# A spectral mixer with a tanh-shrink network: another front for the pipeline, and another way to bound |h|

**Chip, cores, metric.** One core of one Trainium2 chip. The metric is the device time of one execution in microseconds (us), median of several runs. A program on one core has no second die to compare with; all runs told of here were classed as fast.

## The reference

```python
# x: (8, 3008, 256) float32; filt_r, filt_i: (1505, 256) float32
X = np.fft.rfft(x, axis=1)
y = np.fft.irfft(X * (filt_r + 1j * filt_i)[None], n=3008, axis=1).astype(np.float32)
t = y.reshape(24064, 256)
h = t @ w_in                    # w_in: (256, 2048), float64 as it arrives
g = h - np.tanh(h)
out = (g @ w_out).astype(np.float32)   # w_out: (2048, 256), float64
```

## The kernel before

The length 3008 is split as 64 x 47. A batch's transform has a first step (`first`: `x` to `a`, stored to a scratch tensor `ct1`), a middle step (`middle`: `pz`, times the filters into `uv` and `zs`, then `pe`, stored to `ct2`), and a last step (`last`: `pu`, copied into `ut`). The first batch has its own form of these, the **front**. Then the main loop runs 192 units. Each has seven products instead of eight in `up` (h in blocks, by sums of blocks), the shrink function, and seven products in `down`; the sums are made by GpSimd (`combine`). The transforms of later batches are threaded through the loop. TensorE is meant to be busy all the time.

The weights arrive as 64-bit floats, and the kernel rebuilds them from their bits as 32-bit ones, in eight quarters of two jobs each. Five quarters are converted in the front, three in the loop's first units:

```python
def converted(tiles, src, dsts, queue):
    # ... t = raw 64-bit words, loaded on SP
    yield
    V.tensor_scalar(out=it, in0=hi, ...)                 # mantissa bits
    ACT.activation(ft, it, AF.Identity, bias=1.0, scale=2.0 ** -20)
    V.tensor_scalar(out=pt, in0=hi, ...)                 # exponent
    ACT.activation(pt, pt, AF.Relu, bias=exp_b)
    V.tensor_scalar(out=st, in0=hi, ...)                 # sign
    V.scalar_tensor_tensor(out=ft, in0=lo, scalar=2.0 ** -52, in1=ft, ...)
    yield
    V.tensor_scalar_min(pt, pt, 255.0)
    # ... two to four more VectorE operations, into wu or wd

# in the front:
ws = weights(tiles0, range(5), 2)           # advanced by next(ws) in first0 and in each step j
# in the loop:
late, copies = weights(tiles1, range(5, 8), 2), filters_d()
# ...
if k in (0, 2, 4):
    next(late, None)
elif U > 0:
    next(copies, None)                      # 8 x 6 DMAs on SP, filters into a DRAM scratch
```

The shrink uses an approximation that holds for |h| < 0.98. A bound of |h| is computed on the chip, and a general path runs if it fails. The bound is |W|^T max|u|: a reduce after each `last`, and at the end the absolute weights and 64 small matmul passes:

```python
V.tensor_reduce(out=largest[:, :, i:i + 1], in_=ut[:, :, 0:n], axis=X, op=ALU.max,
                apply_absolute_value=True)               # 48 times
# shrink, twice a unit:
ACT.activation(y[k], ht[k], AF.Arctan, scale=S)
ACT.activation(y[k], y[k], AF.Square)
# bounded(), in the last four units and after them:
#   w_abs = |wu[0:2]|, |wu[4] + wu[3]|, |wu[3]|     (ScalarE, VectorE, 8 steps)
#   pb = w_abs^T @ largest ; small = pb < NEAR ; least = min ; count = ones^T @ least
```

`turned`, in the front, prepares the second half of an inverse matrix (`gx`) with two ScalarE operations for each of eight chunks.

Of the kernel before, what the change touches and what calls it, by code (L numbers as in the profile page):

```python
# [41 lines left out]
EARLY = 3  # L42
# [101 lines left out]
def kernel(  # L144
# [32 lines left out]
    largest = cst.tile([128, 2, len(groups)], F32, name="largest")  # L177
# [14 lines left out]
    def converted(tiles, src, dsts, queue):  # L192
# [13 lines left out]
        ACT.activation(ft, it, AF.Identity, bias=1.0, scale=2.0 ** -20)  # L206

        V.tensor_scalar(out=pt, in0=hi, scalar1=20, scalar2=0x7FF,
                        op0=ALU.logical_shift_right, op1=ALU.bitwise_and)
        ACT.activation(pt, pt, AF.Relu, bias=exp_b)  # L210
        V.tensor_scalar(out=st, in0=hi, scalar1=-2 ** 31, scalar2=None, op0=ALU.bitwise_and)
        V.scalar_tensor_tensor(out=ft, in0=lo, scalar=2.0 ** -52, in1=ft,
                               op0=ALU.mult, op1=ALU.add)
        yield
        V.tensor_scalar_min(pt, pt, 255.0)
# [10 lines left out]
    def weights(tiles, quarters, ahead):  # L226

# [21 lines left out]
        def start(k):  # L249
            j = converted(tiles, *jobs[k], nc.sync)  # L250
            next(j)
            return j

        def sums(u):
            w = (wu if u < 4 else wd)[:, :, 256 * (u % 4):256 * (u % 4) + 256]
            G.tensor_sub(w[:, 4], w[:, 6], w[:, 3])
            G.tensor_sub(w[:, 5], w[:, 4], w[:, 0])
            G.tensor_sub(w[:, 2], w[:, 1], w[:, 5])
            G.tensor_sub(w[:, 6], w[:, 0], w[:, 6])

        began = [start(k) for k in range(ahead)]
        yield
        for k in range(len(jobs)):
            next(began[k])
            if k and k % 2 == 0:
                sums(quarters[k // 2 - 1])
            if k + ahead < len(jobs):
                began.append(start(k + ahead))
            yield
            next(began[k])  # L270
            yield
        sums(quarters[-1])
        yield

# [57 lines left out]
    def load_a2(p, j, filters=True):  # L332

        t = tr.tile([RP2, 2 * BD], F32, tag="a2", bufs=2, name="a2")
        row = 32 * len(UNITS[p]) * DM
        nc.sync.dma_start(t, dram(ct1[p], 2 * j * BD, [[row, RP2], [1, 2 * BD]]))
        n = 2 if len(UNITS[p]) == 2 else 4
        if not filters:
            return t
        ft = tr.tile([128, 2, n, DM], F32, tag="ft", bufs=2, name="ft")  # L340
        for p0 in (0, IM):
            nc.sync.dma_start(ft[p0:p0 + IM], dram(filt_d, n * j * DM,
                                                   [[2 * NK * DM, IM], [NK * DM, 2], [1, n * DM]]))
        if n * (j + 1) == NK:
            nc.sync.dma_start(ft[IM:IM + 1, 0, n - 1, :],
                              dram(filt_r.tensor, SEQ // 2 * DM, [[DM, 1], [1, DM]]))
        return t, ft
# [61 lines left out]

    CHUNKS = [chunks_of(bs, CH) for bs in UNITS]  # L410
# [26 lines left out]
    def last(i, z):  # L437
# [7 lines left out]
        for h in range(2):  # L445
# [5 lines left out]
            if h == 0:  # L451
                yield
        V.tensor_reduce(out=largest[:, :, i:i + 1], in_=ut[:, :, 0:n],
                        axis=mybir.AxisListType.X, op=ALU.max, apply_absolute_value=True)
# [73 lines left out]
    def shrink(U):  # L528
# [9 lines left out]
        def start(k):  # L538
            y[k] = tiles("y", 2)
            ACT.activation(y[k], ht[k], AF.Arctan, scale=S)  # L540
            ACT.activation(y[k], y[k], AF.Square)  # L541
# [145 lines left out]
    def bounded(z):  # L687


        ng = len(groups)  # L690
        small = tr.tile([128, 2, NP, ng], F32, tag="a2", bufs=2, name="small")
        ones = cst.tile([128, 1], F32, name="ones")
        G.memset(ones, 1.0)
        w_abs = [tr.tile([128, 2, DFF // 2], F32, tag="ft", bufs=2, name="w_abs")
                 for _ in range(2)]
        for half in range(2):
            for t in range(4):
                cols = slice(t * 256, (t + 1) * 256)
                if half == 0:
                    ACT.activation(w_abs[0][:, :, cols], wu[:, 0:2, cols], AF.Abs)  # L700
                else:
                    V.tensor_add(w_abs[1][:, 0, cols], wu[:, 4, cols], wu[:, 3, cols])
                    ACT.activation(w_abs[1][:, 0, cols], w_abs[1][:, 0, cols], AF.Abs)
                    ACT.activation(w_abs[1][:, 1, cols], wu[:, 3, cols], AF.Abs)
                yield
        for half in range(2):
            pb = z("pb", [128, NP, ng])
            for t in range(NP):
                for h in range(2):
                    nc.tensor.matmul(pb[:, t], w_abs[half][:, h, t * 128:(t + 1) * 128],  # L710
                                     largest[:, h], start=(h == 0), stop=(h == 1),
                                     skip_group_check=True)
                if t == NP // 2 - 1 and half == 0:
                    yield
            V.tensor_single_scalar(out=small[:, half], in_=pb, scalar=NEAR, op=ALU.is_lt)
            if half == 0:
                yield
        least = cst.tile([128, 1], F32, name="least")
        V.tensor_reduce(out=least, in_=small, axis=mybir.AxisListType.XYZ, op=ALU.min)
# [3 lines left out]
        yield  # L723
# [69 lines left out]
    with tc.tile_pool(name="tr", bufs=2) as tr:  # L793
        with tc.tile_pool(name="pro", bufs=1) as pro, \
# [7 lines left out]
            def big(shape, dtype, name):  # L802

                return pro.tile(shape, dtype, tag="big", bufs=4, name=name)
# [35 lines left out]
            def filters_of(c, to=None):  # L840


                n = 4 if c < NK // 4 - 1 else 3

                def put(row, m, v, i, n_s, src, off, dims):
                    if to is None:
                        dst = t[IM * v + row:IM * v + row + m, v, i:i + n_s, :]
                    else:
                        dst = dram(to, ((row * 2 + v) * NK + 4 * c + i) * DM,
                                   [[2 * NK * DM, m], [DM, n_s], [1, DM]])  # L850
                    (G if to is None else nc.sync).dma_start(dst, dram(src.tensor, off, dims))

                if to is None:
                    t = filt[c % 3]


                    if c < 3:
                        for v in range(2):
                            G.memset(t[IM * v + 32:IM * v + 64, v], 0.0)
                    if n == 3:  # L860
                        G.memset(t[IM:IM + 1, 1, 3], 0.0)
                for row, m in ((0, LO), (LO, 16), (LO + 16, HI - 16)):
                    sign = 1 if row < LO else -1
                    r0 = 4 * c + 1 + NQ * row if row < LO else NQ * (row - LO + 1) - 1 - 4 * c
                    for v, src in enumerate((filt_r, filt_i)):
                        put(row, m, v, 0, n, src, r0 * DM, [[NQ * DM, m], [sign * DM, n], [1, DM]])
                if n == 3:
                    for v, src in enumerate((filt_r, filt_i)):
                        put(v, LO - v, v, 3, 1, src, v * NQ * DM,
                            [[NQ * DM, LO - v], [DM, 1], [1, DM]])  # L870
                        put(LO, HI, v, 3, 1, src, NQ // 2 * DM,
                            [[NQ * DM, HI], [DM, 1], [1, DM]])
                return None if to is not None else t
# [8 lines left out]
            def turned(g3, t):  # L882


                ACT.copy(t[0:RP], g3[IM:IM + RP])
                ACT.mul(t[IM:IM + RP], g3[0:RP], -1.0)
# [11 lines left out]
            with tc.manual_schedule():  # L898
                nc.sync.dma_start(wf1, wf1_d)
                V.memset(near_b, B)  # L900
                V.memset(exp_b, -896.0)
                xs = [load_x0(0, (0, 4, 8)), load_x0(1), load_x0(2)]
                ws = weights(tiles0, range(5), 2)

                pad = pro.tile([64, DM], F32, name="pad")
                G.memset(pad, 0.0)
                G.dma_start(dram(ct1[0], NR * 64 * DM, [[DM, 64], [1, DM]]), pad)
                fts = {0: filters_of(0)}
                gx = [pro.tile([IM + RP, 4, RP2], F32, name=f"gx{k}") for k in range(2)]
                for t in gx:  # L910
                    G.memset(t[32:64], 0.0)
                mats = {0: load_slots(0, pro)}
                next(ws)
                for c in range(3):
                    for k, _ in enumerate(first0(xs[c], c)):
                        if k == 3 or k == 1 and c > 0:
                            next(ws)
                G.dma_start(s2, s2_d)
                fts[1] = filters_of(1)
                a2 = {0: load_a2(0, 0, False)}  # L920
                mats[1] = load_slots(1, pro)
                next(ws)
                double_filters(fts[0], 0)
# [216 lines left out]
```

## Time and profile before

| | before |
|---|---|
| median | 2852.3 us |
| TensorE busy | 2744.0 of 2850.8 us (96%) |
| VectorE, ScalarE, GpSimd busy | 70%, 66%, 61% |
| first `pu` matmul (front's end) | 116.3 us |
| unit 0, 8, 188 (the add into `h` from `y`) | 125.3, 262.7, 2775.5 us |

Read the busy rows first, for where TensorE is not full. Then cut the span by stage, and in each stage ask which wait ends last. A unit is marked by its first VectorE add (`h<-y,s`), which occurs once per unit.

### The profile page before, as it was taken

The numbers are of one execution on the slowest core, as the hardware profiler recorded it, in microseconds if no ns is written. First come the engines' busy times: TensorE is split into PE (matmuls) and PEld (weight loads), VectorE is DVE, ScalarE is ACT, GpSimd is POOL, SyncE is SP. The second block draws the span as 40 slices with busy tenths as digits, with TensorE's granted clock in tenths as the row PEclk, the third lists the DMA queues.
The fourth block names the chain that finished last, engine by engine and source line by source line (L and its number), as shares of the span: only waits on it lengthen the run. The fifth ranks groups of instructions, "written<-read, shape, count | busy, mean of one in ns | idle before, by whom it ended". The sixth has DMA issues, their size and how long they took to land.

```text
span 2850.8 us, 36441 instructions
## 1 busy us (share of the span) xinstructions
PE 2744.0 (96%) x12482; PEld 2276.7 (80%) x12482; DVE 1983.7 (70%) x2211; ACT 1871.5 (66%) x2450; POOL 1738.0 (61%) x1381
## 2 busy tenths in 40 slices
PE   5789999999999999999999999999999999999998
PEld 2567777888878887888877788788888888898887
DVE  4675666766766777766776777676687777777876
ACT  3655666666666666666666667666666666666665
POOL 4345777544677767644576776755466666555554
PEclk7989999999999999999999999999999999999999
DMA  9644443232223322132232223212222322111010
GB/s 265 190 152 118 113 113 92 60 93 84 73 67 80 85 73 59 41 98 78 67 99 67 70 71 83 53 39 68 58 65 62 78 55 57 30 19 25 16 22 16
DMA packets 324269, 217.53 MB, mean 76 GB/s; under 512 B 225037, under 2 KB 276485, under 8 KB 323882
## 3 DMA queue, kind: packets, MB, share of 16 engines
q1 hardware_dynamic: 269304, 160.36, 23.1%
q10 hardware_dynamic: 52818, 51.53, 6.0%
q0 software_dynamic: 1952, 3.22, 0.5%
q8 instruction: 100, 1.64, 0.2%
q14 instruction: 95, 0.78, 0.1%
HBM read 138.87 MB, written 79.17 MB: 76 GB/s over the span
## 4 chain that ended last, share of the span: by engine, by line
PE 77%; ACT 8%; DVE 6%; issue 3%; DMA 3%; POOL 1%; SPq 1%; ACTq 1%; DVEq 0%; POOLq 0%
PE o L591 31%; PE x L484 20%; PE z L484 9%; PE y L484 5%; PE pe L365 3%; PE pu L448 3%; PE pz L384 3%; ACT y L540 2%; PE pf L305 2%; DVE h L545 2%; ACT y L541 1%; DVE uv L399 1%; ACT zs L398 1%; ACT u L490 1%; DMA filt<-in_filt_i_dram 1%
## 5 line engine op out<-in xcount | busy, mean ns | idle before, releaser
L591 PE MATMUL o<-t,wd 128*128 128x256 f32 (+2 forms) x3072 | 775.8, 375 | 0.0
L545 DVE TENSOR_TENSOR h<-h,y 128x1024 f32<-128x1024 f32 (+2 forms) x384 | 582.1, 1516 | 258.1 <-ACT y L541 258.1
L591 PEld LDWEIGHTS o<-t,wd 128*128 128x128 f32 x3072 | 580.6, 190 | 71.7
L484 PE MATMUL x<-tu,wu 128*128 128x256 f32 (+2 forms) x2304 | 591.6, 379 | 18.4 <-ACT u L490 16.9
L549 DVE SCALAR_TENSOR_TENSOR h<-sq,h 128x1024 f32<-128x1024 f32 (+2 forms) x384 | 569.9, 1484 | 20.8 <-ACT y L540 0.5
L463 POOL TENSOR_TENSOR t<-h 128x512 f32<-128x512 f32 (+2 forms) x192 | 240.7, 1253 | 558.9 <-DVE h L549 495.9
L591 PE MATMUL o<-h,wd 128*128 128x256 f32 (+2 forms) x2304 | 581.1, 375 | 0.2 <-DVE h L549 0.2
L484 PEld LDWEIGHTS x<-tu,wu 128*128 128x128 f32 x2304 | 429.4, 191 | 161.5 <-issue 73.3
L591 PEld LDWEIGHTS o<-h,wd 128*128 128x128 f32 x2304 | 430.9, 190 | 70.9 <-issue 19.1
L546 ACT ACTIVATE sq<-y,near_b 128x1024 f32<-128x1024 f32 (+2 forms) x384 | 435.4, 1134 | 6.1 <-DVE h L549 1.4
L540 ACT ACTIVATE y<-h 128x1024 f32<-128x1024 f32 (+2 forms) x384 | 400.0, 1042 | 14.8 <-ACT e L368 7.6
L541 ACT ACTIVATE y<-y 128x1024 f32<-128x1024 f32 (+2 forms) x384 | 399.3, 1040 | 12.2
L490 ACT COPY s<-x 128x512 f32<-128x512 f32 (+2 forms) x192 | 110.8, 577 | 439.8 <-PE x L484 431.2
L466 POOL TENSOR_TENSOR t<-t,h 128x512 f32<-128x512 f32 (+2 forms) x192 | 308.8, 1608 | 0.1
L490 ACT COPY u<-x 128x512 f32<-128x512 f32 (+2 forms) x384 | 219.4, 571 | 68.6 <-PE x L484 33.3
L464 POOL TENSOR_TENSOR t<-h,t 128x512 f32<-128x512 f32 (+2 forms) x192 | 241.7, 1259 | 15.1
L465 POOL TENSOR_TENSOR t<-h 128x512 f32<-128x512 f32 (+2 forms) x191 | 250.2, 1310 | 0.0
L400 POOL TENSOR_TENSOR zs<-zs,ft 128x512 f32<-128x512 f32 x112 | 165.9, 1481 | 117.4 <-ACT zs L398 117.3
L401 POOL TENSOR_TENSOR uv<-uv,zs 128x512 f32<-128x512 f32 x112 | 214.9, 1919 | 15.6 <-DVE uv L399 7.2
L484 PE MATMUL x<-ut,wu 128*128 128x256 f32 (+2 forms) x768 | 198.8, 381 | 8.1 <-DVE h L520 6.5
L500 DVE TENSOR_TENSOR h<-y,s 128x512 f32<-128x512 f32 (+2 forms) x192 | 130.2, 678 | 96.2 <-PE y L484 86.0
L484 PE MATMUL z<-tu,wu 128*128 128x256 f32 (+2 forms) x768 | 194.5, 376 | 0.1
(120 smaller groups left out, 3289.1 us busy)
## 6 DMA issues: line engine op xcount, KB each, us to landing
a<-ct SPq DMA_DIRECT2D x64, 384.0 KB
ct<-e ACTq DMA_DIRECT2D x128, 192.0 KB
ft<-filt SPq DMA_DIRECT2D x96, 256.0 KB
out_dram<-ot SPq DMA_DIRECT2D x1392, 16.0 KB
ct<-a ACTq DMA_DIRECT2D x80, 256.0 KB
x_sb<-in_x_dram SPq DMA_DIRECT2D x69, 256.0 KB
e<-ct SPq DMA_DIRECT2D x33, 512.0 KB
fg<-fg SPq DMA_DIRECT2D x40, 392.0 KB
```

Of the source, the lines that this page charges most:

```text
L463: G.tensor_sub(t[0], b[0][1], b[0][0])
L464: G.tensor_sub(t[1], b[1][1], t[0])
L465: (V if shared else G).tensor_sub(t[2], b[1][1], b[0][1])
L466: G.tensor_sub(t[3], t[1], b[1][0])
L484: nc.tensor.matmul(bank[:, k], wu[:, q - 1, (2 * u + k) * 128:(2 * u + k + 1) * 128], rhs[q - 1], start=(first and k == 0), stop=True, ski ...
L490: ACT.copy(t, X)
L540: ACT.activation(y[k], ht[k], AF.Arctan, scale=S)
L541: ACT.activation(y[k], y[k], AF.Square)
L545: V.tensor_mul(ht[k], ht[k], y[k])
L546: ACT.activation(sq[k], y[k], AF.Square, bias=near_b, scale=A)
L549: V.scalar_tensor_tensor(out=ht[k], in0=sq[k], scalar=K, in1=ht[k], op0=ALU.add, op1=ALU.mult)
L591: nc.tensor.matmul(product(q), wd[:, q - 1, (2 * u + k) * 128: (2 * u + k + 1) * 128], rhs[q - 1][:, k], start=(u == 0 and k == 0 and q == ...
```

## The change

Its intent: the front is one that a sibling kernel uses. VectorE converts three quarters alone, before the first batch's middle step; three more follow in the steps; the last two come in the loop in small steps, with ScalarE's part one step behind VectorE's. `turned` moves to GpSimd, the filters' copies to GpSimd in ten DMAs (the largest of 744 rows of 1 KB), `e` gets four buffers, one early `first` step fewer. And |h| is bounded by the sums of y = arctan(S h)^2 that ScalarE's accumulator gives beside the squares: if every sum is under arctan(S 0.98)^2, every |h| is under 0.98. The diff below is cut; it leaves out, among other things, that `a2` is loaded a chunk further ahead and that one hand-written order of instructions now spans the whole program, where the front and the loop had one each.

```diff
-EARLY = 3
+EARLY = 2
@@ converted(..., alone=False)
         V.tensor_scalar(out=it, in0=hi, scalar1=0xFFFFF, ...)
-        ACT.activation(ft, it, AF.Identity, bias=1.0, scale=2.0 ** -20)
         V.tensor_scalar(out=pt, in0=hi, scalar1=20, ...)
-        ACT.activation(pt, pt, AF.Relu, bias=exp_b)
         V.tensor_scalar(out=st, in0=hi, scalar1=-2 ** 31, ...)
+        yield
+        if alone:
+            V.tensor_scalar(out=ft, in0=it, scalar1=2.0 ** -20, scalar2=1.0, ...)
+            V.tensor_scalar(out=pt, in0=pt, scalar1=-896.0, scalar2=0.0, ...)
+        else:
+            ACT.activation(ft, it, AF.Identity, bias=1.0, scale=2.0 ** -20)
+            ACT.activation(pt, pt, AF.Relu, bias=exp_b)
+        yield
# ... (more yields; weights() interleaves two jobs; weights_alone(), weights_slow() are new)
@@ the front
-                ws = weights(tiles0, range(5), 2)
+            ws = weights_alone(tiles0, range(3))
# ...
+            a2[1] = load_a2(0, 1, False, "ft")
             double_filters(fts[0], 0)
+            for _ in ws:
+                pass
+            ws = weights(tiles0, range(3, 6), 2)
@@ turned
-                ACT.copy(t[0:RP], g3[IM:IM + RP])
-                ACT.mul(t[IM:IM + RP], g3[0:RP], -1.0)
+                G.tensor_copy(t[0:RP], g3[IM:IM + RP])
+                G.tensor_scalar_mul(t[IM:IM + RP], g3[0:RP], -1.0)
@@ the loop
-                for c in range(NK // 4):
-                    filters_of(c, filt_d)                # six DMAs each, on SP
+                for v, row, m, i, n, src in filter_rows(0, NK):
+                    G.dma_start(dram(filt_d, ...), src)  # ten DMAs in all
                     yield
-            late, copies = weights(tiles1, range(5, 8), 2), filters_d()
+            late, copies = weights_slow(tiles1, range(6, 8)), filters_d()
@@ the bound
-        V.tensor_reduce(out=largest[:, :, i:i + 1], in_=ut[:, :, 0:n], ...)
-            ACT.activation(y[k], y[k], AF.Square)
+            ACT.activation(y[k], y[k], AF.Square,
+                           accum_out=y_sums[:, 2 * U + k // 2:2 * U + k // 2 + 1])
-        # w_abs, pb: eight steps of ScalarE and VectorE, 32 matmuls
+        V.tensor_single_scalar(out=small, in_=y_sums, scalar=float(np.arctan(S * NEAR) ** 2),
+                               op=ALU.is_lt)
+        V.tensor_reduce(out=least, in_=small, axis=mybir.AxisListType.X, op=ALU.min)
         pc = z("pc", [1, 1])
         nc.tensor.matmul(pc, least, ones, start=True, stop=True)
# called in unit total + 1, k == 0: between the last products
```

## The prediction

> **What bounds the kernel now.** I read the page's busy shares and forty slices first. They show where TensorE is short of its best.
>
> ```profile
> PE 2744.0 (96%) x12482; PEld 2276.7 (80%) x12482; DVE 1983.7 (70%) x2211; ACT 1871.5 (66%) x2450; POOL 1738.0 (61%) x1381
> ...
> PE   5789999999999999999999999999999999999998
> ...
> PEclk7989999999999999999999999999999999999999
> DMA  9644443232223322132232223212222322111010
> ```
>
> TensorE is busy 2744.0 of 2850.8 us, so all its idle time is 106.8 us. It lies in the first slices and the last one (a slice is 71 us). The clock is below full only there too. I then cut the span by stage in the view of windows: the front of batch 0 (0 to 119 us; the first `pu` matmul starts at 119.0), the first units of the main loop, the middle, and the tail.
>
> ```profile
> 0.00:44.00 44.00, 16.82 (x26) 6.00 (x26) 12.05 (x26) 14.59 (x24) 18.19 (x33) 0.82 0.93 271
> 44.00:103.00 59.00, 48.58 (x178) 32.24 (x178) 46.26 (x89) 37.17 (x56) 32.88 (x54) 0.87 0.90 233
> 103.00:119.00 16.00, 9.27 (x29) 5.24 (x29) 1.26 (x3) 4.00 (x7) 1.89 (x3) 0.83 0.58 177
> 119.00:262.00 143.00, 124.84 (x493) 96.48 (x494) 98.64 (x125) 83.22 (x112) 59.36 (x55) 0.91 0.47 143
> 262.00:500.00 238.00, 222.55 (x909) 166.03 (x908) 144.44 (x161) 162.41 (x223) 186.44 (x133) 0.99 0.41 106
> 500.00:2780.00 2280.00, 2263.55 (x10530) 1916.30 (x10529) 1635.49 (x1754) 1534.47 (x1978) 1409.84 (x1083) 1.00 0.25 62
> 2780.00:2850.80 70.80, 58.42 (x324) 54.43 (x322) 45.52 (x57) 35.62 (x54) 29.43 (x25) 0.95 0.08 16
> ```
>
> The columns are the stretch, its length, busy time of PE, PEld, DVE, ACT and POOL, granted clock, DMA share, GB/s. From 500 to 2780 us TensorE idles 16.5 us in 2280. It is the bound there, and nothing that VectorE, ScalarE or GpSimd is spared there can buy more than that. In the first 103 us the sixteen DMA engines are 90 to 93% busy: the front is held by transfers, with waits of ScalarE and VectorE among them. From 119 to 262 us TensorE idles 18.2 us and runs at 0.91 of its clock. That is the softest place.
>
> The waits of the front name the culprits. Columns: who waited, for whom, us in total, times, longest.
>
> ```profile
> DVE conv L205 <- DMA raw<-in_moe_w_in_dram: 21.6, 1, 21.6
> ACT conv L206 <- DVE conv L205: 16.5, 4, 7.9
> PE pf L828 <- ACT a L831: 9.5, 2, 5.8
> PE pz L952 <- DMA a<-ct: 9.3, 1, 9.3
> ACT a L306 <- PE pf L305: 6.8, 2, 6.4
> ```
>
> ScalarE takes its work in order. It stands at the first conversion, which waits for raw weights that land at 22.5 us, and only then copies batch 0's `pf` out of PSUM.
>
> From 105 to 300 us the waits of TensorE and of the SP queue say the same of the late quarters:
>
> ```profile
> PE x L484 <- ACT u L490: 12.5, 5, 3.8
> PE pf L305 <- DMA x_sb<-in_x_dram: 10.9, 4, 5.4
> ...
> SPq L198 <- DVE ft L212: 30.6, 4, 12.4
> SPq L851 <- DMA ct<-a: 24.1, 7, 6.6
> ```
>
> SP stands behind raw loads whose buffer isn't free and behind the filters' copies (L851). The `x` loads queue behind them. ScalarE's `u` copies stand behind conversions.
>
> **What the Trainium skill says.** (1) "TensorE: Matmul & The Clock Gate", Part 1: an idle window drops the array to half clock, and it must be busy some 3.4 us to get it back. The trace agrees: x4 matmul groups of 1.03 us take 2.07 us after the 3.61 us wait at 141 us. The mean clock 0.987 means some 2 x 0.0125 x 2851 = 71 us at half clock, nearly all before 281 us. (2) "DMA: Bandwidth & Descriptors", "Issuing engines are not separate DMA queues": transfers from SP, ScalarE and GpSimd share the same 16 engines, so moving an issue saves only time on the issuing queue. The front's 0.90 to 0.93 fits, so I count nothing for bytes. (3) "ScalarE: Activation LUTs", "What ACT_TABLE_LOAD costs": an ACTIVATE costs 186 ns + 0.833 ns per element, 93 ns more with a pointer bias. For 1024 elements 1039 and 1132 ns; the trace has 1040 (L541) and 1134 (L546). The page says an accumulator output exists, but no price; no row of before shows one. (4) "Perfetto Trace Analysis", "DMA Instruction — SWDGE (GPSIMD)": GpSimd's part of a DMA is writing descriptors. Its filter loads here take 0.56 us each (L851), with 28 to 96 rows of 1 KB alike.
>
> **The change part by part.**
>
> *First stage on VectorE alone.* Six of sixteen half-quarter conversions no longer use ScalarE (two activations, 0.63 + 0.71 us each, out of ten such in the old front). VectorE gets two more simple passes of 0.43 us. One job is then 5 x 0.43 + 2 x 0.69 + 0.76 = 4.3 us of VectorE without a hand-over. ScalarE's `pf` copies no longer wait: of the 9.5 us wait most goes, and `a<-ct` can start some 8 us earlier. But the six jobs take 6 x 4.3 = 26 us of VectorE after the first raw weights land at 22.5, so its first `uv` comes at about 49 to 50 us against 46.2 now. The early start is largely given back there.
>
> *The middle of batch 0.* It holds 6 conversions instead of 7, `turned` leaves ScalarE (8 x 1.03 us) for GpSimd, `e` gets four buffers for two (11.1 us of ScalarE waits for `ct<-e`), and `a2` is loaded a step earlier. Steps now take 59/16 = 3.7 us. When nothing waits they take 3.0 (pz and pe of 84 to 91 us). 16 x 3.1 from 50 us ends at about 100. DMA load rises by one quarter, 1 MB, some 4 us at 250 GB/s. So I count 2 us here, not 8.
>
> *The gap from 103 to 119.* The third early `first` step waits for `x_sb` (5.4 us), then for a buffer of `a1`, and ScalarE stands with it (`ACT ut L450 <- DMA ct<-a` 2.2 us). With EARLY = 2 and the loads begun a step earlier this goes: 7 us. Front together: **9 us** (0 to 15).
>
> *The loop's first units.* Two quarters instead of three come late, in small steps in which ScalarE's part is issued one step after VectorE's. The filters' copies, 48 issues and more on SP, become 10 on GpSimd. What there is to win from 119 to 300 us: idle 24 us, and clock: 34 us at half clock, of which some 28 busy, cost 14. Together 38. GpSimd's ten issues, if 0.6 to 3 us, are 6 to 30 us of an engine busy 59 of 143 us there. I take 40% of 38: **15 us** (5 to 25).
>
> *The bound.* Before: 48 reduces of 1.22 us on VectorE (59 us), 64 matmuls and 8 steps of absolute weights. After: an accumulator read after each of 384 squares. Estimated at 0.1 to 0.25 us each from the fixed part of an activation, that is 40 to 95 us of ScalarE, taking it from 1535/2280 = 67% to some 70%. Both lie beside TensorE. VectorE's release and the lengthened chain `y` to `h` (258 us of waits by VectorE, hidden) about cancel: **0** (-5 to +5).
>
> *The tail.* In the timeline, two batches of 16 `pb` matmuls stand between `o` products, and 32 more stand behind the last transposes:
>
> ```profile
> 2825.15 1.88 PE L710 MATMUL pb<-largest,w_abs 128*128 128x48 f32 x16
> 2828.45 1.88 PE L710 MATMUL pb<-largest,w_abs 128*128 128x48 f32 x16
> 2837.91 3.67 PE L710 MATMUL pb<-largest,w_abs 128*128 128x48 f32 x32
> 2843.54 0.15 DVE L722 CAST count<-pc 1x1 int32<-1x1 f32 x1 [0.37 <-PE pc L721]
> ```
>
> The first two give back up to 3.8 us. The last output transfer is issued at 2838.9 and needs about 2.3 us to land (the 256 KB `ct<-a` on the chain of waits take 2.14 to 2.58), so to 2841.2; the count comes at 2843.7. The count is ready earlier in the new one, so 2.5 us more. Without `w_abs` between 2786 and 2803, where TensorE idles about 3 us, 2 us more. Together **8 us** (5 to 11).
>
> Sum: 9 + 15 + 0 + 8 = 32, so 2852 - 32 = 2820 us, 1.1% faster.
>
> **The rivals.** *The front stays on DMA*: engines are already over 90% busy and 1 MB is added, so the front gains nothing, or loses 5. For it: the DMA row. Against: from 103 to 119 DMA is at 0.58, so the end of the front isn't full. Then some 2830 to 2834. *GpSimd becomes the bound* of the first units: it takes the copies' descriptors (744 rows each in the large ones, not measured here), `turned` and the usual combines, and TensorE waits for `t`. For it: POOL is busy 186 of 238 us from 262 on. Against: copies are done before, where it is busy 59 of 143. Then 2835. *The accumulator costs in the steady state*: ScalarE's `u` copies come late behind 0.25 us reads twice a unit; 192 units x 0.1 us would lose 19 us and give 2840. Against: all of TensorE's waits on `u` from 300 to 2800 us are 4.4 us. *Everything soft goes*: front 15, loop 38, tail 11 would give 2788, faster by over 2%; this needs no wait to take another's place, which I doubt.
>
> **Range and chances.** The steady 2280 us can't shrink by more than 16.5 us, so over 2% (below 2795) needs nearly all of front, loop and tail: 5%. Slower by 2% would need 57 us lost in parts that are beside TensorE: 2%. Range 2802 to 2840.
>
> **What would show it.** The first `pu` at 106 to 116 us instead of 119; ScalarE with no wait on `conv` in first0; DVE's first `uv` at about 50. From there the seventh unit's end some 15 us nearer the start, with fewer half-clock stretches. No row for `pb`; the tail from the last `o` product to the end shorter by over 2 us. A row for accumulator reads on ScalarE of 0.1 to 0.25 us x384, and TensorE from 500 us on still 99% busy. I'm wrong if TensorE's idle time in the middle grows (accumulator), if GpSimd's copies hold `t`, or if the first `pu` isn't earlier.

## The result

The changed kernel takes 2840.6 us (2837.8 to 2842.6, six runs) against 2852.3 for the kernel before in the same rounds. The ratio is 0.9956, with a 95% interval of 0.9944 to 0.9969. A ratio is the mean time of one kernel's fast runs over that of the other's of the same rounds, so it is not quite the ratio of the medians. It is a gain of 12 us, not of 32; the time lies just above the range.

The same stages of the changed kernel, in the view of windows (columns as in the prediction):

```profile
44.00:103.00 59.00, 41.76 (x152) 28.45 (x150) 50.41 (x94) 26.35 (x36) 44.53 (x66) 0.82 0.95 235
103.00:119.00 16.00, 12.36 (x42) 8.44 (x42) 3.29 (x7) 5.59 (x8) 5.13 (x7) 0.82 0.47 134
119.00:262.00 143.00, 128.50 (x518) 100.27 (x519) 84.13 (x108) 89.48 (x133) 69.92 (x65) 0.91 0.57 162
...
500.00:2768.00 2268.00, 2252.45 (x10472) 1904.86 (x10471) 1563.29 (x1701) 1548.48 (x2293) 1430.67 (x1076) 1.00 0.26 63
```

From 44 to 103 us TensorE did less than before (41.8 us busy against 48.6), and GpSimd is now the second busiest there (44.5 against 32.9). A window at fixed times can't show which stage gained, because the stages have shifted. So I put the marks of both profiles side by side:

| stage, by marks in the two profiles | before | changed | difference | predicted |
|---|---|---|---|---|
| start to unit 0 (front) | 125.3 | 129.7 | +4.4 | -9 |
| unit 0 to 8 | 137.4 | 123.2 | -14.2 | -15 |
| unit 8 to 188 | 2512.8 | 2516.7 | +3.9 | 0 |
| unit 188 to the end | 75.3 | 69.9 | -5.4 | -8 |
| sum | 2850.8 | 2839.5 | -11.3 | -32 |

The loop's first units did what was said of them. The front missed its forecast by 13 us, the middle (unit 8 to 188) and the tail by 3.9 and 2.6.

In the front of the changed kernel, TensorE's waits from 44 to 126 us are these, first by its matmuls, then by its weight loads:

```profile
PE pe L957 <- DVE uv L983: 10.3, 5, 6.4
PE pu L511 <- DMA e<-ct: 5.9, 1, 5.9
PE pe L959 <- DVE wd L230: 5.3, 1, 5.3
...
PEld pe L959 <- POOL gx L899: 5.7, 1, 5.7
```

The first line is the largest: 6.4 us of it are the wait for the first `uv`. VectorE's own waits for its `uv` in this stretch are put down to ScalarE, which doubles the filters:

```profile
DVE uv L983 <- ACT filt L889: 10.8, 5, 5.2
```

The third and the last line of the first view are one and the same wait, put down to two engines. The product needs `gx` (L899 is `turned`), and the weight load names it rightly; VectorE's `wd` only feeds what stands ahead on GpSimd. GpSimd's own timeline (start, duration, instruction) shows the queue:

```profile
97.34 0.51 POOL L885 DMA_DIRECT2D filt<-in_filt_i_dram  x1 [0.51 <-DMA filt<-in_filt_i_dram]
97.92 0.72 POOL L260 TENSOR_TENSOR wd<-wd 128x256 f32<-128x256 f32 x1
...
100.21 1.17 POOL L263 TENSOR_TENSOR wd<-wd 128x256 f32<-128x256 f32 x1
101.44 0.58 POOL L898 COPY gx<-fg 48x384 f32<-48x384 f32 x1
102.10 1.50 POOL L899 TENSOR_SCALAR gx<-fg 48x384 f32<-48x384 f32 x1
```

TensorE is ready for `gx` at 98.4 us and goes on at 103.66. Until then GpSimd issued filter loads, some of which wait for earlier ones to land, and made the sums of a quarter of weights.

### The profile page after: what moved, and what is told of

Its sections match the earlier page's. It is cut to its first block, busy times and chain, and to the rows that moved or that the text cites. A ratio compares the mean times of both kernels' runs of the same rounds, so it can differ in the third digit from the quotient of the medians.

```text
span 2839.5 us, 36615 instructions
## 1 busy us (share of the span) xinstructions
PE 2734.4 (96%) x12418; PEld 2270.6 (80%) x12418; DVE 1910.9 (67%) x2170; ACT 1881.9 (66%) x2794; POOL 1794.4 (63%) x1407
## 4 chain that ended last, share of the span: by engine, by line
PE 77%; ACT 9%; issue 5%; DVE 4%; POOL 1%; ACTq 1%; DMA 0%; DVEq 0%; SPq 0%; POOLq 0%
PE o L653 31%; PE x L545 20%; PE z L545 9%; PE y L545 5%; PE pe L411 3%; PE pu L511 3%; ACT y L601 3%; PE pz L430 3%; PE pf L351 2%; DVE h L607 1%; ACT u L551 1%; ACT zs L444 1%; ACT y L602 1%; DVE uv L445 1%; ACT zs L443 1%
## 5 line engine op out<-in xcount | busy, mean ns | idle before, releaser
L607 DVE TENSOR_TENSOR h<-h,y 128x1024 f32<-128x1024 f32 (+2 forms) x384 | 570.4, 1485 | 279.6 <-ACT y L602 279.6
L653 PEld LDWEIGHTS o<-h,wd 128*128 128x128 f32 x2304 | 431.2, 190 | 71.3 <-issue 18.8
L602 ACT ACTIVATE y<-y 128x1024 f32<-128x1024 f32 (+2 forms) x384 | 399.2, 1040 | 12.2
L575 DVE TENSOR_TENSOR h<-z,u 128x512 f32<-128x512 f32 (+2 forms) x192 | 129.5, 674 | 171.1 <-ACT u L551 168.2
```

The lines of the kernel that those rows point to most:

```text
L602: ACT.activation(y[k], y[k], AF.Square, accum_out=y_sums[:, 2 * U + k // 2:2 * U + k // 2 + 1])
L607: V.tensor_mul(ht[k], ht[k], y[k])
L653: nc.tensor.matmul(product(q), wd[:, q - 1, (2 * u + k) * 128: (2 * u + k + 1) * 128], rhs[q - 1][:, k], start=(u == 0 and k == 0 and q == ...
```

## The experiments

All kernels gave correct results. The marks come from the one profile of each; the ratio is to the kernel before, of the same rounds, with its 95% interval.

| run | first uv | last e | first pu | unit 0 | unit 8 | unit 188 | end | median | ratio |
|---|---|---|---|---|---|---|---|---|---|
| before | 46.2 | 106.6 | 116.3 | 125.3 | 262.7 | 2775.5 | 2850.8 | 2852.3 | 1 |
| changed | 52.0 | 114.3 | 121.9 | 129.7 | 252.9 | 2769.6 | 2839.5 | 2840.6 | 0.9956 (0.9944-0.9969) |
| e1_turned_scalar | 51.7 | 111.8 | 118.9 | 126.2 | 249.3 | 2767.2 | 2835.5 | 2836.8 | 0.9931 (0.9919-0.9943) |
| e2_uv_first | 44.1 | 111.6 | 118.7 | 127.2 | 251.0 | 2766.2 | 2834.4 | 2837.2 | 0.9935 (0.9923-0.9947) |
| e3_five_quarters | 53.1 | 114.0 | 120.5 | 128.9 | 258.6 | 2777.4 | 2847.6 | 2847.4 | 0.9967 (0.9955-0.9978) |
| e4_ones_early | 53.1 | 115.1 | 122.9 | 130.8 | 254.2 | 2772.5 | 2840.6 | 2841.4 | 0.9947 (0.9935-0.9959) |
| e5_no_accum | 52.3 | 114.4 | 121.9 | 129.3 | 250.5 | 2758.0 | 2829.0 | 2830.1 | 0.9910 (0.9894-0.9926) |
| e6_bound_alone | 45.7 | 107.6 | 117.5 | 125.8 | 265.3 | 2782.0 | 2852.1 | 2853.2 | 0.9991 (0.9977-1.0006) |
| e7_copies_sp | 52.7 | 115.1 | 122.5 | 130.6 | 258.9 | 2775.1 | 2845.2 | 2842.8 | 0.9958 (0.9944-0.9972) |
| e8_late_two_steps | 51.7 | 114.4 | 121.8 | 129.8 | 261.1 | 2778.0 | 2848.2 | 2848.8 | 0.9977 (0.9964-0.9990) |
| e9_front_both | 45.1 | 104.3 | 110.6 | 118.9 | 241.7 | 2757.8 | 2828.7 | 2832.1 | 0.9926 (0.9913-0.9940) |
| e10_tail_last | 52.0 | 113.3 | 119.8 | 128.3 | 252.2 | 2770.0 | 2836.9 | 2838.7 | 0.9947 (0.9933-0.9961) |
| e11_best | 44.7 | 105.2 | 111.6 | 120.0 | 244.1 | 2761.8 | 2828.5 | 2830.5 | 0.9916 (0.9903-0.9930) |
| e12_extra_mb | 44.1 | 105.9 | 112.2 | 119.9 | 243.3 | 2761.3 | 2828.0 | 2831.0 | 0.9924 (0.9910-0.9937) |

"Last e" is ScalarE's last copy of a `pe` of batch 0. Runs that leave the front as it is show how far one profile's front can be trusted: in e4, e5, e7, e8 and e10 the first `pu` lies between 119.8 and 122.9 us. Differences of 1 to 2 us in the front are no finding.

### e1_turned_scalar

```diff
-                G.tensor_copy(t[0:RP], g3[IM:IM + RP])
-                G.tensor_scalar_mul(t[IM:IM + RP], g3[0:RP], -1.0)
+                ACT.copy(t[0:RP], g3[IM:IM + RP])
+                ACT.mul(t[IM:IM + RP], g3[0:RP], -1.0)
```

> The changed kernel with the two operations of `turned` back on ScalarE (8 x 1.03 us there, against 8 x 1.86 us on GpSimd). Theory G (GpSimd became the bound of the front: `turned` stands behind filter issues and sums, and TensorE waits 5.25 us for gx at 98.4 us): that wait goes, the first pu comes 4 to 6 us before the 121.9 of the changed kernel, and the time is 2834 to 2837. Theory V (six conversions on VectorE ahead of the first uv set the front) and theory D (the DMA engines, 92 to 95% busy for 103 us, set it): first pu within 2 us of 121.9, time 2838 to 2842.

The 5 us wait for `gx` goes; what is left of it, in TensorE's waits of this run, is five short ones:

```profile
PE pe L959 <- ACT gx L899: 2.8, 5, 0.6
```

The first `pu` comes 3.0 us earlier, less than the 4 to 6 expected of theory G, and the time falls to 2836.8. Part of the gain went to another wait: TensorE's waits for `uv` rise from 10.3 to 14.0 us, with one of 4.7 us at 92 us, after ScalarE's conversion has waited 4.5 us for raw weights. So GpSimd was one bound of the front, but not the only one.

### e2_uv_first

```diff
-            for _ in ws:
-                pass
-            ws = weights(tiles0, range(3, 6), 2)
             next(ws)                        # the 4th of six early jobs; two more in j = 0, 1
# ... in the loop over j:
+                if j == 1:
+                    for _ in ws:
+                        pass
+                    ws = weights(tiles0, range(3, 6), 2)
+                    next(ws)
```

> The changed kernel with only four of the six early conversions ahead of the first uv; the other two follow the first two steps. Bytes and engines are the same. Theory V: the first uv comes at 43 to 45 us instead of 52.0, and first pu 4 to 8 us before 121.9; time 2833 to 2837. Theory D: first uv earlier, but first pu within 2 us of 121.9, as the transfers pace the steps that follow. Theory G: the same, the 5 us wait for gx stays or grows.

The first `uv` comes at 44.1 us as expected, 7.9 us earlier. The first `pu` comes only 3.2 us earlier. It falls between the theories: the early start is worth something, but the steps after it lose more than half of it again, with `gx` still on GpSimd (waits of 4.1 us).

### e3_five_quarters

```diff
-            ws = weights(tiles0, range(3, 6), 2)
+            ws = weights(tiles0, range(3, 5), 2)
-            late, copies = weights_slow(tiles1, range(6, 8)), filters_d()
+            late, copies = weights_slow(tiles1, range(5, 8)), filters_d()
                     next(late, None)
+                    if U == 3:
+                        next(late, None)
```

> The changed kernel with five quarters of weights converted in the front instead of six (three on VectorE alone, two in the steps), and three late in small steps. 1 MB, some 4 us of all DMA engines, leaves the front. Theory D: first pu 3 to 5 us earlier than 121.9. Theory V: the first uv is unchanged at 52, first pu within 2 us. Theory G: one set of sums less on GpSimd ahead of the last gx (3.5 us), first pu 3 to 5 us earlier too; the row of DMA busy share tells it from D. The loop's first eight units then carry a third quarter and take up to 5 us more, so the total is 2837 to 2842 in any case.

One megabyte less in the front moved the last `e` by 0.4 us and the first `pu` by 1.5, within the spread. Theory D predicted 3 to 5. So did theory G, for one set of sums less on GpSimd, and that isn't seen either: TensorE still waits 6.3 us for `gx` here. The bytes did leave: the DMA share from 44 to 103 us is 0.88 here against 0.95. The late third quarter costs units 0 to 8 6.5 us (129.7 against 123.2), and the total is worse by some 7 us, beyond the range that I gave. The sixth quarter in the front is a good part of the change.

### e4_ones_early

```diff
-        G.memset(ones, 1.0)                 # in bounded(), at the end
+            V.memset(ones, 1.0)             # at the start
```

> The changed kernel with the one memset of `ones` moved from the bound at the end (where it stands on GpSimd behind the last combines, and TensorE waits 2.4 us for it in the middle of its last products, then falls to half clock) to the start, on VectorE. Theory: the wait goes and with it the half clock, so 3 to 4 us less: 2836 to 2838. Rival (the end waits for the combines of the last unit anyway): under 1 us.

A miss. It gained nothing in time that shows (2841.4; ratio 0.9947 with an interval that overlaps the changed kernel's), and the tail's 68.1 us instead of 69.9 are no gain of its own, since e1 and e2, with the changed kernel's tail, have 68.3 and 68.2. The wait for `pc` went from 2.40 to 1.95 us, now for VectorE's reduction: one wait took the place of the other. The half clock after it, at 2826 us, was absent here, but also in the profiles of e1 and e2, which have the same tail as the changed kernel, so it isn't tied to `ones`.

### e5_no_accum

```diff
-            ACT.activation(y[k], y[k], AF.Square,
-                           accum_out=y_sums[:, 2 * U + k // 2:2 * U + k // 2 + 1])
+            ACT.activation(y[k], y[k], AF.Square)
+            V.memset(y_sums, 0.0)           # once: the bound is then always met
```

> The changed kernel without the accumulator output of the squares; the sums are set to zero once, so the bound is always met (on purpose; right for these inputs). In all five profiles of the changed form the units 24 to 188 take 2243.2 to 2243.8 us, against 2239.3 before. Theory A (the 384 accumulator reads of 186 ns on ScalarE hold the copies that TensorE waits for): 2239 to 2240 again, and some 4 us off the total. Rival B (the reads are hidden beside TensorE; the loss comes from elsewhere, such as VectorE running ahead without the reduces): 2243 again, total unchanged.

The clearest of all: 2830.1 us, 10.5 us less than the changed kernel, and more than the 4 of theory A. Units 24 to 188 take 2236.3 us against 2243.3 in the changed kernel, which is 7.0 less; the rest comes from the units before 24 (2.0 us in units 0 to 8, 2.2 in 8 to 24). The kernel before takes 2239.3 for them. So the accumulator reads cost 7.0 us in that stage; that the missing reduces give back 3.0 is the difference between this run and the kernel before, with no run of its own.

The reads have a row of their own on ScalarE in the changed kernel:

```profile
L602 ACT ACTIVATION_READ_ACCUMULATOR y<-y 128x1 f32 x384 | 71.5, 186 | 0.0
```

Their records overlap with others: between the marks of units 24 and 188 ScalarE's busy time is 1532.9 us with the reads and 1506.5 without, some 0.08 us for each of 328. That is an engine busy 66% of the time, and yet TensorE pays. The waits of its weight loads (PEld) and matmuls (PE) from 530 to 2750 us for ScalarE's `u` copies show how: before, changed, and without the reads:

```profile
PEld x L484 <- ACT u L490: 16.6, 36, 1.0
PE x L484 <- ACT u L490: 3.1, 7, 0.6
```

```profile
PEld x L545 <- ACT u L551: 27.2, 62, 1.1
PE x L545 <- ACT u L551: 7.7, 22, 0.7
```

```profile
PEld x L545 <- ACT u L551: 17.1, 38, 1.0
PE x L545 <- ACT u L551: 3.1, 7, 0.6
```

The weight loads have 62 waits instead of 36, and 38 once the reads are gone; 10 us more and then 10 us less. They overlap with running matmuls; the matmuls' own waits rise by 4.6 us and fall by as much. The `u` copies stand behind the read in ScalarE's order, and TensorE's next product waits for `u`.

### e6_bound_alone

The kernel before with only the bound changed (the diff's last part; no other).

> The kernel before with the new bound alone (sums from the accumulator, no reduces, no absolute weights, no products of them), the old front and the old late quarters. If the parts are independent: first pu at 116 to 117 and units 0 to 8 in 137 us as before, units 24 to 188 in 2243 to 2244, units 188 to 191 in 33.3 instead of 37.4, and a total of 2849 to 2852: the bound alone is worth nothing. If its loss in the middle comes only together with the new front, the middle is 2239 and the total 2845 to 2847.

The middle is 2243.7 us as expected, the tail from unit 188 to 191 33.3 (37.4 before), units 0 to 8 139.5 (137 expected), and the whole 2853.2 us, ratio 0.9991, just above the 2849 to 2852 expected. The new bound alone is worth nothing: what it saves in the tail and on VectorE it loses on ScalarE. That the same loss shows in the old front's company says that the two halves of the change are independent in the middle.

### e7_copies_sp and e8_late_two_steps

```diff
# e7_copies_sp: the filters' copies on SP again, in 8 x 6 pieces and more
-                    G.dma_start(dram(filt_d, ...), src)
+                        nc.sync.dma_start(dram(filt_d, ...), src)
# e8_late_two_steps: the late quarters in the front's coarser order
-            late, copies = weights_slow(tiles1, range(6, 8)), filters_d()
+            late, copies = weights(tiles1, range(6, 8), 2), filters_d()
-                    next(late, None)
+                    if k in (0, 2, 4):
+                        next(late, None)
```

> The changed kernel with the filters' copies back on SP in eight times six pieces. Theory S (the loop's first units gained because SP is free for the loads of x): units 0 to 8 take 129 to 137 us instead of 123.2. Rival T (they gained because the late quarters are fewer and in small steps): 123 to 125, total as the changed kernel.

> The changed kernel with its last two quarters issued in the front's coarser order (two conversions interleaved, three issues a unit) instead of one small step at each place. Theory T: units 0 to 8 take 127 to 133 us instead of 123.2. Theory S: 123 to 125.

Units 0 to 8 take 128.3 us in the first and 131.3 in the second, against 123.2: 5.1 us for the copies, 8.1 for the small steps, together 13.2 of the 14.2 gained. Each theory holds for a part. The sum is no proof that nothing else counts: the third late quarter alone cost 6.5 us (e3), so the parts overlap. With the copies on SP, that queue (119 to 262 us) waits again behind ScalarE's stores:

```profile
SPq L1036 <- DMA ct<-a: 18.5, 7, 7.4
```

With the coarser steps, a raw load of weights stands on SP until its buffer is free, and TensorE waits for the `x` loads behind it (the SP queue's wait first, then TensorE's, same stretch):

```profile
SPq L197 <- DVE ft L219: 16.2, 1, 16.2
```

```profile
PE pf L351 <- DMA x_sb<-in_x_dram: 7.5, 2, 6.2
```

The steps show in the time too (2848.8). The copies do not: 2842.8, ratio 0.9958, the same as the changed kernel within the interval; its profiled run was slower than its median. So the 5 us are seen in one profile's stage and aren't shown for the whole.

### e9_front_both

Both edits of e1 and e2 together.

> The changed kernel with both mends of the front: `turned` on ScalarE and four conversions instead of six ahead of the first uv. Alone they brought the first pu from 121.9 to 118.9 and to 118.7. If GpSimd and VectorE each held other steps (theory G + V), the gains add: first pu at 115 to 117, loss against the kernel before gone, total 2831 to 2834. If the DMA engines hold what is left (theory D), first pu stays at 118 to 119 and the total at 2834 to 2837.

The first `pu` comes at 110.6 us: 11.3 earlier than in the changed kernel, against 3.0 and 3.2 for the edits one by one, and earlier than expected. The gains don't just add: with one edit, the other engine is still in the way of the same steps. It is 5.7 us earlier than in the kernel before, and unit 0 6.4 us earlier. The time is 2832.1, as expected. The ratios of e1, e2 and e9 have intervals that overlap; that both edits are worth more than one is shown by these marks, which e11 and e12 repeat (111.6 and 112.2), not by the ratio.

### e10_tail_last

```diff
+        yield                               # VectorE's part at k == 0 of the last unit
         nc.tensor.matmul(pc, least, ones, start=True, stop=True)
         V.tensor_copy(count, pc)
# ... its second part runs after the last products and transposes; ones set early as in e4
```

> The changed kernel with the count's one small matmul issued after the last products and transposes instead of in their midst, and the constant set early. With the constant alone moved, TensorE waited 1.95 us there instead of 2.40, for VectorE's reduction. Theory (the place in TensorE's order costs it): no wait for `pc`; from the last unit's first add to the end 33 to 34 us, against 34.8 to 37.7 in the profiles so far; 1.5 to 3 us off the total. Rival: the count's way into the register then ends last and nothing is gained.

In the changed kernel, TensorE's timeline of the tail has the one small matmul `pc` in the midst of the products, with its wait, and the products behind it at half speed:

```profile
2817.22 1.40 PE L653 MATMUL o<-t,wd 128*128 128x224 f32 x6 [1.29 <-POOL t L526]
...
2820.11 1.78 PE L653 MATMUL o<-h,wd 128*128 128x224 f32 x8
2824.28 0.19 PE L760 MATMUL pc<-ones,least 128*1 128x1 f32 x2 [2.40 <-POOL ones L755]
...
2826.11 4.03 PE L653 MATMUL o<-t,wd 128*128 128x224 f32 x14
```

With `pc` last it waits for nothing, and the x14 group takes 2.81 us. It does so in e1, e2 and e4 too, with `pc` in the midst: the half clock follows it in seven of ten profiles, and in none of the three with `pc` last.

```profile
2823.31 2.81 PE L653 MATMUL o<-t,wd 128*128 128x224 f32 x14
...
2827.68 0.19 PE L759 MATMUL pc<-ones,least 128*1 128x1 f32 x2
```

From unit 191 to the end it is 33.6 us, against 36.6 in the changed kernel's profile and 34.8 to 37.7 in the others with `pc` in the middle (34.8 to 35.0 in the three at full clock). The time, 2838.7, is 2 us better, too little to show in the intervals; the place in TensorE's order is shown by the timeline.

### e11_best and e12_extra_mb

e11 has the edits of e9 and e10. e12 adds a megabyte of transfers to it:

```diff
+                if j in (2, 6):             # batch 0's middle: 4 x 256 KB, DRAM to DRAM, on SP
+                    nc.sync.dma_start(dram(spare, ...), dram(x.tensor, ...))   # twice
```

> Both mends of the front and the mended tail together. If they are independent: first pu as in the run with both mends of the front, end as in the run with the mended tail; total 2829 to 2833, faster than both kernels.

> The run with all mends, with 1 MB more moved by the DMA engines in the front (four copies of 256 KB from the input to a spare tensor, issued on SP at steps 2 and 6 of batch 0's middle; the results are not used). It doubles the suspected cost D: one more quarter of weights. Theory D (transfers set the mended front): first pu 4 to 6 us later than without. Theory G + V: within 2 us.

e11 runs in 2830.5 us, ratio 0.9916 (0.9903 to 0.9930): faster than the kernel before by 0.8% and than the changed kernel by some 0.4%, with intervals that don't meet. It has the lowest median of the versions here that really check their bound (e9's interval overlaps with its own).

The extra megabyte moves the first `pu` by 0.6 us and the time by 0.5. In the windows of the two runs (44 to 104 us) it shows as more GB/s, last column, with the DMA engines at 0.86 to 1.01 in the column before it. First without, then with:

```profile
44.00:74.00 30.00, 25.55 (x89) 17.81 (x88) 24.95 (x51) 15.34 (x23) 16.10 (x28) 0.81 0.99 256
74.00:104.00 30.00, 24.98 (x99) 16.64 (x98) 26.27 (x50) 21.96 (x33) 16.53 (x25) 0.94 0.94 233
```

```profile
44.00:74.00 30.00, 23.68 (x88) 15.97 (x88) 26.42 (x53) 15.76 (x24) 17.41 (x30) 0.90 1.01 270
74.00:104.00 30.00, 25.65 (x95) 17.51 (x94) 24.13 (x47) 20.98 (x31) 14.93 (x24) 0.87 0.86 245
```

A DMA share of 0.9 to 1.0 did not mean that bytes set the pace: a megabyte more was carried at 245 to 270 instead of 233 to 256 GB/s. Theory D is refuted for this front, in this order of issue, and for a megabyte of this kind (DRAM to DRAM; for a quarter of weights there is e3). VectorE, busy 51.2 of 60 us there, is now the fullest engine, just ahead of TensorE (50.5).

## Why the prediction was wrong

**What bounds the kernel.** Right as far as it went: the middle is TensorE's, and what could be won lay in the front, the first units and the tail. Two readings were wrong. "The front is held by transfers" was read off the DMA row; e3 and e12 say no. And I gave the first `pu` as 119.0 us; that is its second group, the first starts at 116.3. "TensorE from 500 us on still 99% busy" came true (2252.45 of 2268 us) while the middle got longer: between the marks of units 24 and 188, with 10336 matmuls in both profiles, TensorE's busy time went from 2225.5 to 2227.8 us and its idle time from 13.8 to 15.6, neither of which shows in a share of 99%. The distance between marks shows it, and the growing idle time was among my signs of being wrong.

**The front, "9 us (0 to 15)", was the step that failed.** It measured +4.4 at unit 0. Of its three parts:

- *First uv "at about 49 to 50 us"*: 52.0. Nearly right, and rightly set against the early start. I treated it as the price of the change; e2 shows that it was not needed.
- *"16 x 3.1 from 50 us ends at about 100"*: the last `e` comes at 114.3, so the steps took (114.3 - 52.0)/16 = 3.9 us, not 3.1. This is the term that broke: 62.4 us for sixteen steps instead of 49.6. I took the length of steps that wait for nothing and gave it to steps that do. One of their waits, 5.3 us, is the one for `gx`: I counted `turned` as ScalarE's relief and did not ask what it would stand behind on GpSimd: filter issues and the sums of weights, 44.5 us busy of 59. GpSimd's two operations take 0.62 + 1.24 us against 0.51 + 0.52 on ScalarE. I named GpSimd as a rival, but for the wrong stage (the loop, where its ten issues cost only 0.5 to 0.7 us each). What e1 (the wait goes), e2 and e9 show is that `turned` on GpSimd and the late first `uv` cost the front its gain: with both mended, the first `pu` comes 5.7 us before that of the kernel before, and unit 0 6.4 us, inside the 0 to 15 that I had claimed. But the steps still take 3.7 us there, from 45.1 to 104.3, so most of this term's error is explained by neither. What the trace shows of the rest: where the changed kernel's steps run evenly, two of them take 6.8 us (ScalarE's `e1s` copies at 56.48, 63.31, 70.08 and 76.86 us). In each pair ScalarE copies a result, does its two operations of a conversion and then doubles the filters, for which the next `uv` waits. No run moved the conversions from there, so this cause is read from the trace and not shown.
- *The gap, "7 us"*: from the last `e` to the first `pu` it went from 9.6 to 7.6 us, so 2. The wait on the third early step went, and a wait for the `e<-ct` load (5.9 us) took its place. The load can't start early: it is issued at 117.59 us, 2.6 us after the last `ct<-e1s` store (114.95), for which its queue waits, and TensorE goes on at 121.94. A store and a load through DRAM, 7.0 us here and 5.7 in e9, stand between the last `e` and the first `pu`, so 7 of the 9.6 us were never to be had. That the load's part is slow because the late quarters' loads share the moment was not tested.

**The rival "the front stays on DMA"** would have given 2830 to 2834 and looked best by the DMA row. e3 and e12 say no.

**The first units, 15 us: right.** 14.2 measured, from its named causes: the small steps by e8 (8.1), one late quarter less by e3 (6.5) and the copies by e7 (5.1, which shows in the stage alone). They overlap, and "40% of 38" was a guess, so that the number is met so closely is partly luck.

**The bound in the middle, "0 (-5 to +5)"**: +3.9 from unit 8 to 188, inside its bracket, but I held that the two sides "lie beside TensorE" and would cancel. They don't lie beside it. The reads' length was well guessed (186 ns, in 0.1 to 0.25), and one of my rivals had the mechanism exactly: the `u` copies come late behind the reads. Its 2840 is what was measured (2840.6), but by luck: it took 19 us from the middle, and the front took most of what was lost. I set it aside because all of TensorE's waits for `u` were 4.4 us; the weight loads' waits for it, 18.8 us from 300 to 2800 in the same profile, might have told more. By e5, the reads cost 10.5 us over the whole kernel, 7.0 of it in units 24 to 188, where the change as a whole loses 4.0.

**The tail, "8 us (5 to 11)"**: 5.4 in this profile, and 7.0 and 7.1 in e1 and e2, which have the same tail without the half clock. The absolute weights were worth more than I took them for (units 188 to 191 fell by 4.1 us, I said 2). The two groups of `pb` were worth less than their 3.8 us, since behind them TensorE waits for GpSimd's `t` anyway (1.29 + 0.53 us, once they are gone). And the new `pc` stands in the midst of the products with 2.4 us of waiting. By e10 and e4, the place of `pc` costs this, not the memset it was seen to wait for; with `pc` last (e10 to e12) the tail is 66.7 to 66.9 us, 8.4 to 8.6 less than before.

What stays open: what holds the mended steps at 3.7 us; why the two mends of the front give 11.3 us together and 6.2 one by one, beyond the argument that each alone leaves the other's wait standing; and whether the copies' move to GpSimd gains anything in the whole time.

## What to carry to other kernels

An operation that is moved to an idler engine is served in that engine's order: look at what will stand ahead of it, not at the engine's share. A small, regular addition to an engine that is a third idle isn't free where another engine waits for what stands behind it; the waits of matmuls and of weight loads for that thing show the price (3.1 to 7.7 us and 16.6 to 27.2 us here). Price stages by the distance between marks that both kernels have, and put a lone bookkeeping matmul after the last products, not among them.

## What the Trainium skill lacked or had wrong

- "ScalarE: Activation LUTs": it says that an ACTIVATE can give an accumulator output, but not what it costs. Here each is a second instruction, ACTIVATION_READ_ACCUMULATOR, of 186 ns (71.5 us for 384), of which some 0.08 us each adds to ScalarE's busy time; the ACTIVATE itself stays at 1040 ns. The kernel lost 10.5 us by them (e5_no_accum).
- "DMA: Bandwidth & Descriptors", "Anatomy of one DMA — SWDGE (gpsimd) path", calls descriptor generation "small, variable" and gives no time. GpSimd's part of a copy took 0.58 and 0.52 us with 744 rows, 0.68 and 0.69 with 496, and 0.51 to 0.79 with 21 to 96 rows in the front: here it didn't grow with the rows.
- "GPSIMD Engine Reference", section 3, compares with VectorE only. For 48 x 384 elements: 0.62 us for a copy and 1.24 us for a multiplication by a constant on GpSimd, against 0.51 and 0.52 us on ScalarE.
- "TensorE: Matmul & The Clock Gate", Part 1, gives half clock after an idle window of about 3.4 us. Here it followed a shorter wait, of 2.4 us, in six of the eight profiles that have that wait before `pc`: the x14 group behind it took 3.14 to 4.03 us, against 2.81 in the other two (e1 and e2). What decides between them isn't shown.
